# Batch 0's last direct units, earlier up heads and spread transposes in an attention and feed-forward kernel

## The chip, the core and the metric

The kernel runs on one core of a Trainium2 chip. Its time is the device time in microseconds of one execution; several executions give a median. A core has five engines that each run their own list of instructions in order: TensorE (PE, matrix products; PEld is its loading of weights), VectorE (DVE), ScalarE (ACT), GpSimd (POOL) and SyncE (SP). An instruction starts once the instructions of other engines that it depends on are done. Transfers are issued by SP, POOL and ACT, and are carried out by 16 DMA engines.

## The reference

```python
# attention: u, v are (8, 3008, 256), z is (8, 3008, 64)
scores = (1.0 / S) * np.matmul(z, z.transpose(0, 2, 1))
attn = np.maximum(scores, 0.0) ** 2
out = u * np.matmul(attn, v)
# feed-forward: x is out as (24064, 256); w_in is (256, 2048), w_out (2048, 256)
h = x @ w_in
g = h * (1.0 / (1.0 + np.exp(-1.702 * h)))
return g @ w_out
```

There is no softmax: the attention weights are the squares of the positive scores. Since the scores are z times z transposed, the matrix of weights is symmetric.

## The kernel before

A batch has 3008 rows: 24 blocks of 128, the last a half. Four blocks make a chunk of 512 queries, so there are six chunks, i = 0 to 5, the last of 448.

**Scores.** A unit (i, jp) is the score tile of chunk i's queries with two blocks of keys: two matmuls (`scores`, L222), then relu on ACT into `rl` (L246), then the square on DVE into `a` (L260). The tiles `sc` have two buffers in PSUM, which the up groups' `hg` share (the tag `ps2`); `rl` has three buffers, `a` has 21, and the left sums `s` of the feed-forward take theirs from the same 21. In batches 1 to 7 the first unit on a chunk's diagonal writes at L251, and the second (`folded`) is half as wide and writes to `ad` at L244.

**Symmetry.** Only units with keys at or behind the chunk's own are computed. For a later chunk the same square is turned by a DMA transpose from SP (`turn_unit`, L267) into a tile `tt`, one for each pair of chunks. For the last chunk it is done the other way (`turned`, L218): the unit is computed with chunk 5's 512 queries and transposed for the earlier chunk. Where `turned` is false, chunk i computes its units with chunk 5 directly, and chunk 5 computes its own. In batch 0, before, chunks 0 to 2 are direct and chunks 3 and 4 turned.

**Attention.** `attend` (L298) gives a chunk's work as a list of 47 slots, n = 0 to 46. A slot is one or two matmuls `o` with V (L330). In most chunks there are two passes over the blocks, with a slot for the last half block between them (n = 23); there POOL has an empty instruction (`post`, L83) that waits for the first pass and that the second pass waits for. The result is multiplied by the turned u at L347 (`gate`) and is the input `xt` of the feed-forward.

**The order of work** is written by hand: every instruction is placed by the loop over b, i and n at L616 to L648. `SCHED0`, `SCHED`, `SCHED_LAST` and `NEXT` say at which slots of which chunk units are taken from the queue. Chunk 5 of a batch already takes units of the next batch's chunk 0 (`NEXT`). `TURN0` and `TURN` say at which slots u is turned by DVE (L201), `LOAD0` and `LOAD` at which slots POOL issues a load of u; a tile `uq` of u has two buffers, so a load waits for the turning of u two chunks back. `LOADW` places the loads of the weights W1 (L409) and W2 (L412), on POOL as well, and `load_z` the next batch's z, whose cast on POOL waits for its own landing (L160).

**Feed-forward.** An up group (`up_group`, L364) is four matmuls into `hg`, ACT's function into `gf` (L379, two buffers), and a scaling into `gt` on DVE (L383). There are 48 a batch; the first 18 (`LAGY`, the heads) stand between the slots of chunk 4 (chunk 5 in the last batch), the rest each with one product of the down part, `product` (L457), whose outputs SP stores. The down part multiplies by a seven-product scheme, for which DVE forms sums of `gt` (L435) and, in batch 0, sums of W2 (`weight_sums`, L414), one or two after each up group. The tiles `gt` and `tt` share 15 buffers.

**The late transposes.** The transposes of the next batch's chunk 0 units taken in chunk 5 are not issued there but kept in `late`. They are issued after the up groups, one or two after each of the products that remain. The two units taken last are not kept.

Of the kernel before, what the change touches and what calls it, by code (L numbers as in the profile page):

```python
# [15 lines left out]
def kernel(  # L16
# [20 lines left out]
    NJ = (S + P - 1) // P  # L37
# [3 lines left out]
    NCH = (S + CH - 1) // CH  # L41
    CB = CH // P
# [34 lines left out]
    late, LATE = [], []  # L77
# [12 lines left out]
    def behind(sig, m):  # L90
        tc.add_manual_dep(m.ins, sig.ins.name, SYNC, reason="row tiles of one bank")
# [92 lines left out]
    def width(i):  # L184
        return CH if i < NCH - 1 else LAST
# [31 lines left out]

    def turned(b, i):  # L218

        return i < NCH - 1 and (b > 0 or i > 2)  # L220

    def scores(b, group):  # L222
        scs = []
# [53 lines left out]
    def weights(b, i, j):  # L277

        cj, g = divmod(j, CB)
        n = NCH - 1  # L280
        if n in (i, cj) and not turned(b, min(i, cj)):
            return unit[b, i, j // 2][:, j % 2, :width(i)]
        if i < n and cj == n:
            return TT[b, i, n][:, :, g, :]
        if folded(b, i) and cj == i:
            return unit[b, i, j // 2][:, :, g % 2, :]
        if i == n and cj < n:
            return unit[b, cj, NU - 2 + g // 2][:, g % 2, :LAST]
        if cj >= i:
            return unit[b, i, j // 2][:, j % 2, :width(i)]  # L290
        return TT[b, cj, i][:, :, g, :]


    def full(b):

        return NCH - 2 if b < B - 1 else NCH - 1

    def attend(b, i, both=False):  # L298


        n = width(i)
        js, cs = list(range(NJ - 1)), range(2)
        own = i * CB
        if b == 0 and i in (3, 4):
            js = js[own:-CB + 1] + js[:own] + js[-CB + 1:]
        elif b and i == NCH - 3:
            js = js[own:own + 2] + js[own + CB:-CB + 1] + js[:own] + js[own + 2:own + CB] + js[-CB + 1:]
        elif b and i < NCH - 2:
            js = js[own:own + 2] + js[own + CB:-CB + 1] + js[own + 2:own + CB] + js[:own] + js[-CB + 1:]
        half = [(0, TOP, NJ - 1), (1, LOW, NJ - 1)]  # L310
        if both:
            order = [[(c, FULL, j)] for j in js[:-CB] for c in cs] + [[(c, FULL, j)] for c in cs for j in js[-CB:]]
            order.insert(-CB, half)
        elif i == full(b):
            order = [[(c, FULL, j)] for c in cs for j in js]
            order.insert(0 if i == NCH - 1 else len(order), half)
        else:
            order = [[(0, TOP, j), (1, LOW, j)] for j in js] + [half] + [[(1, TOP, j), (0, LOW, j)] for j in js]
        flat = [(k, m) for k, ms in enumerate(order) for m in ms]
        first = {c: next(m for m in flat if m[1][0] == c) for c in cs}  # L320
        final = {c: [m for m in flat if m[1][0] == c][-1] for c in cs}
        acc, turn = {}, -1 if both or i == full(b) else NJ

        def step(k):
            done = []
            for m in order[k]:
                c, h, j = m
                if (k, m) == first[c]:
                    acc[c] = ps1.tile([P, CH], F32, name="o", tag="ps1")
                ins = pe.matmul(  # L330
                    acc[c][:, :n], V16[b][h, j].rearrange("p (c k) -> p k c", k=NCC)[:, c], weights(b, i, j)[h],
                    start=(k, m) == first[c], stop=(k, m) == final[c],
                )
                if k == turn:
                    behind(acc["sig"], ins)
                done.append(ins)
            if k == turn - 1:
                acc["sig"] = post(done)
            for c in cs:
                if k == final[c][0]:  # L340
                    gate(c)

        def gate(c):
            ut = UT[b, i][:, c].rearrange("p q t -> p (q t)")
            x = XT[b, i]
            if i < NCH - 1 or b % 2:
                dve.tensor_tensor(x[:, c, :n], acc[c][:, :n], ut[:, :n], ALU.mult)  # L347
            else:
                dve.tensor_tensor(x[:, c, :LFULL], acc[c][:, :LFULL], ut[:, :LFULL], ALU.mult)
                dve.tensor_tensor(XT[b + 1, i][:, c, LAST:], acc[c][:, LFULL:n], ut[:, LFULL:n], ALU.mult)  # L350

        XT[b, i] = XT.get((b, i)) or pa.tile([P, NCC, CH], F16, name="xt", tag="xt", bufs=6)
        if i == NCH - 1 and b % 2 == 0:
            XT[b + 1, i] = pa.tile([P, NCC, CH], F16, name="xo", tag="xo")
        return [lambda k=k: step(k) for k in range(len(order))]
# [182 lines left out]
            store(b, k, pool)  # L538

    LAGY = 2 * NFG + 2  # L540
    HEAD, HEAD0 = 2, 8

    def pieces(b, i):

# [5 lines left out]
        k = max(len(lst) - 6, 2)  # L550
        return lst[:k] + lst[-2:] + lst[k:-2]

    NEXT = {n: 1 for n in (1, 6, 11, 16, 32, 36, 40, 44)} | {NJ: 2}
    SCHED = {
        0: {n: 1 for n in (4, 8, 12, 16, 20, 28, 32, 36, 40, 44)} | {NJ: 2},
        1: {n: 1 for n in (2, 7, 12, 17)} | {NJ: 2},
        2: {n: 1 for n in (2, 7, 12, 17)} | {NJ: 2},
        3: {n: 1 for n in (6, 14, 32, 38)} | {NJ: 2},
        4: {},
        5: NEXT,  # L560
    }
# [1 line left out]


    TURN0 = {(i, (38, 28)[i] if i < 2 else NJ + 4 if i < NCH - 1 else 12): i for i in range(NCH)}
    LOAD0 = {(i, n): i + 2 for i, n in TURN0 if i + 2 < NCH}
    TURN = {(1, NJ + 4): 2, (2, NJ + 4): 3, (4, NJ + 4): 4, (5, 8): 5}
    LOADW = {(3, 22): 0, (3, 30): 1, (3, 38): 2, (3, 46): 3, (4, 16): 4, (4, 22): 5, (4, 28): 6, (4, 34): 7}
    LOAD = {(3, NJ + 20): 4, (4, NJ + 5): 5}
# [3 lines left out]
        0: {2: 1, 6: 2, 14: 2, 22: 2, 30: 2, 38: 2},  # L573
        1: {0: 2, 8: 2, 15: 2, 22: 2, 30: 2, 38: 2},
        2: {n: 1 for n in (0, 3, 7, 11, 28, 32, 36, 40, 44)} | {NJ: 2},
        3: {n: 1 for n in (3, 7, 11, 15, 19, 28, 32, 36, 40)} | {NJ: 2},
        4: {},
        5: NEXT,
    }
# [7 lines left out]
    def fill(b):  # L587
        assert not queue
        queue.extend(u_ for i in range(NCH) for u_ in pieces(b, i))
# [26 lines left out]
    for b in range(B):  # L616
        nup = NCH * NFG
        more = b + 1 < B
        sched = SCHED0 if b == 0 else SCHED if more else SCHED_LAST
        turn, load = (TURN, LOAD) if b else (TURN0, LOAD0)  # L620
        head, first = 0, HEAD0 if b == 0 else HEAD
        for i in range(NCH):
            host = b + 1 if more and i == NCH - 1 else b
            if host > b:
                fill(host)
                LATE.append(host)
            for n, step in enumerate(attend(b, i, b == 0 and i < 2)):
                if b == 0 and i == 0 and n == 5:
                    load_u(0, 0)
                if b == 0 and i == 0 and n == 3:  # L630
                    turns[1]()
                if b == 0 and i == 0 and n in FIRST_CAST:
                    first_cast(FIRST_CAST[n], True)
                if b == 0 and i == 0 and n in FIRST_ZT:
                    first_zt(FIRST_ZT[n])()
                if (i, n) in turn:
                    turn_u(b, turn[i, n])
                if (i, n) in load:
                    load_u(b, load[i, n])
                if b == 0 and (i, n) in LOADW:  # L640
                    load_w(LOADW[i, n])
                if more and (i, n) == (NCH - 2, 2):
                    load_z(b + 1)
                take(host, sched[i].get(n, 0))
                if i == full(b) and n >= first and (n - first) * LAGY // (2 * NJ - 2 - first) >= head and head < LAGY:
                    up_group(b, head)
                    head += 1
                step()  # L648
        if more:
            for i in range(2):  # L650
                load_u(b + 1, i)
            for n0 in range(0, NJ, VB):
                load_v(b + 1, n0)
        prods = products(nst(b))
        for q in range(head, nup):
            if more and q in (head + 14, head + 20):
                k = int(q == head + 20)
                turn_u(b + 1, k)
                load_u(b + 1, k + 2)
            up_group(b, q)  # L660
            product(b, *prods.pop(0))
        steps = [lambda kp=kp: product(b, *kp) for kp in prods]
        if nst(b) < NCH:
            k = NCH - 1
            steps += [lambda s=s: down(b, k, s) for s in range(blocks(b)[k][1] // P)]
        late.sort(key=lambda t: t[0])
        for step in steps:
            step()
            if SUMS:
                SUMS.pop(0)()  # L670
            for _, turn_it in [late.pop(0) for _ in range(min(len(late), 1 + (len(steps) < 10)))]:
                turn_it()
        LATE.clear()
        if more:
            while late:
                late.pop(0)[1]()
            take(b + 1, 2)
# [30 lines left out]
```

## Time and profile before

| what | value |
|---|---|
| median of 10 executions | 1214.15 us (1208.6 to 1219.31) |
| the profiled execution | 1209.69 us, its span 1207.9 us |
| DVE busy, ACT busy | 823.4 us, 822.4 us |
| `o` matmuls (L330) with `a`, with `tt` | 300.8 us, 235.4 us |
| up matmuls (L371) | 354.7 us |
| down matmuls (L472) | 93.0 + 92.3 + 91.0 us in the three largest groups |
| score matmuls (L232) | 684, 122.1 us |
| transposes `tt` from SP | 234, 3.8 us from issue to landing (median) |
| DMA share in 60 to 90 us, in 120 to 150 us | 0.83, 0.24 |

The page first gives the busy time of each engine and its share of the span. A row of a timeline has the start in us, the duration, the engine, the line, the operation with output and input, and how many equal instructions are drawn together; in brackets stands how long the engine was idle before and what ended that. A row of the waits has the waiting engine and line, what it waited for, the total in us, how many times, and the longest. The durations of matmuls overlap, so a stretch is measured from start to start. A batch takes about 148 us; batch 0 runs from 0 to 170 us with chunk 4 from 65.7, and chunk 5 of batch 1 starts at 242.8.

### The profile page before, as it was taken

The numbers are of one execution on the slowest core, as the hardware profiler recorded it, in microseconds if no ns is written. First come the engines' busy times: TensorE is split into PE (matmuls) and PEld (weight loads), VectorE is DVE, ScalarE is ACT, GpSimd is POOL, SyncE is SP. The second block draws the span as 40 slices with busy tenths as digits, with TensorE's granted clock in tenths as the row PEclk, the third lists the DMA queues.
The fourth block names the chain that finished last, engine by engine and source line by source line (L and its number), as shares of the span: only waits on it lengthen the run. The fifth ranks groups of instructions, "written<-read, shape, count | busy, mean of one in ns | idle before, by whom it ended". The sixth has DMA issues, their size and how long they took to land.

```text
span 1207.9 us, 27521 instructions
## 1 busy us (share of the span) xinstructions
PE 1187.5 (98%) x11423; PEld 715.5 (59%) x11423; DVE 823.4 (68%) x1321; ACT 822.4 (68%) x977; POOL 230.1 (19%) x325
## 2 busy tenths in 40 slices
PE   9998999999999999999999999999999999999998
PEld 3445774467754676446764468544776547855577
DVE  6677855678757785577775778547786577654776
ACT  7776864677646786477864777647876578663785
POOL 5143100331003310123101231013210132101000
PEclk9999999999999999999999999999999999999999
DMA  9987279862898629966299562994539945497012
GB/s 228 188 109 119 74 160 159 98 100 82 153 162 90 111 71 178 155 69 110 71 187 158 60 110 89 193 143 68 91 95 196 137 76 87 116 184 129 1 36 72
DMA packets 375134, 142.33 MB, mean 118 GB/s; under 512 B 317536, under 2 KB 368480, under 8 KB 375008
## 3 DMA queue, kind: packets, MB, share of 16 engines
q1 hardware_dynamic: 316368, 97.30, 44.3%
q0 software_dynamic: 57280, 42.03, 23.0%
q8 instruction: 89, 1.46, 0.5%
q10 hardware_dynamic: 1360, 1.25, 0.3%
q14 instruction: 37, 0.30, 0.1%
HBM read 60.29 MB, written 24.64 MB: 70 GB/s over the span
## 4 chain that ended last, share of the span: by engine, by line
PE 91%; DMA 4%; ACT 2%; DVE 1%; POOL 1%; issue 1%; DVEq 0%; ACTq 0%; POOLq 0%
PE o L330 35%; PE hg L371 26%; PE st L472 23%; PE sc L232 5%; DMA tt<-a 2%; PE yp L528 2%; ACT rl L246 2%; DMA zst<-in_z_dram 1%; DMA W<-in_moe_w_out_dram 1%; DVE a L260 1%; PE w L97 0%; POOL W L412 0%; POOL uq L194 0%; DVE ut L201 0%; ACT ZT L141 0%
## 5 line engine op out<-in xcount | busy, mean ns | idle before, releaser
L379 ACT ACTIVATE gf<-hg 128x1024 f32<-128x1024 f32 (+1 forms) x384 | 385.7, 1004 | 147.0 <-PE hg L371 126.3
L246 ACT ACTIVATE rl<-sc 128x1024 f16<-128x1024 f32 x307 | 302.1, 1026 | 154.7 <-PE sc L232 131.8
L330 PEld LDWEIGHTS <-V 64*128 64x128 f16 (+1 forms) x4052 | 233.2, 94 | 242.9 <-issue 12.5
L371 PE MATMUL hg<-xt,W 128*128 128x512 f16 (+1 forms) x1408 | 354.7, 375 | 1.6 <-DMA W<-in_moe_w_in_dram 0.9
L383 DVE TENSOR_SCALAR gt<-gf 128x1024 f16<-128x1024 f32 (+1 forms) x328 | 231.2, 705 | 134.7 <-ACT gf L379 132.3
L330 PE MATMUL o<-a,V 64*128 64x512 f16 (+3 forms) x2272 | 300.8, 368 | 0.0
L260 DVE TENSOR_TENSOR a<-rl 128x1024 f16<-128x1024 f16 x272 | 186.8, 695 | 149.6 <-ACT rl L246 144.4
L194 POOL DMA_DIRECT2D uq<-in_u_dram x188 | 125.2, 674 | 633.0 <-PE sc L232 299.0
L330 PE MATMUL o<-tt,V 64*128 64x512 f16 (+1 forms) x1524 | 235.4, 377 | 2.7 <-DMA tt<-a 2.6
L371 PEld LDWEIGHTS <-W 128*128 128x128 f16 x1536 | 139.6, 98 | 125.3 <-issue 3.8
L472 PEld LDWEIGHTS <-gt 128*128 128x128 f16 x2816 | 169.1, 98 | 30.4
L472 PEld LDWEIGHTS <-s 128*128 128x128 f16 x2112 | 127.1, 98 | 22.9
L232 PE MATMUL sc<-ZT 64*128 64x512 f16 (+1 forms) x684 | 122.1, 367 | 10.5 <-ACT rl L246 8.7
L472 PE MATMUL st<-WT,gt 128*128 128x128 f16 x1408 | 93.0, 219 | 0.0
L472 PE MATMUL st<-W,gt 128*128 128x128 f16 x1408 | 92.3, 219 | 0.0
L472 PE MATMUL st<-WT,s 128*128 128x128 f16 x1408 | 91.0, 219 | 0.0
L232 PEld LDWEIGHTS <-ZT 64*128 64x128 f16 x684 | 39.9, 94 | 59.6 <-issue 24.3
L488 DVE SCALAR_TENSOR_TENSOR y<-st,uP 128x256 f32<-128x256 f32 x132 | 55.2, 418 | 27.9 <-ACT uP L482 16.6
L482 ACT ACTIVATE uP<-st 128x256 f32<-128x256 f32 x132 | 49.8, 377 | 33.6 <-PE st L472 22.1
L347 DVE TENSOR_TENSOR xt<-o,ut 128x512 f16<-128x512 f32 x80 | 51.4, 684 | 22.8 <-PE o L330 22.8
L447 DVE TENSOR_TENSOR s<-gt,s 128x1024 f16<-128x1024 f16 x88 | 59.6, 681 | 0.0
L445 DVE TENSOR_TENSOR s<-s,gt 128x1024 f16<-128x1024 f16 x88 | 59.6, 682 | 0.0
(51 smaller groups left out, 615.7 us busy)
## 6 DMA issues: line engine op xcount, KB each, us to landing
out_dram<-y SPq DMA_DIRECT2D x40, 512.0 KB, 3.6
uq<-in_u_dram POOLq DMA_DIRECT2D x156, 128.0 KB, 4.3
V<-in_v_dram POOLq DMA_DIRECT2D x35, 256.0 KB, 6.5
tt<-a SPq DMA_TRANSPOSE x234, 3.8
uq<-in_u_dram POOLq DMA_DIRECT2D x32, 112.0 KB, 5.2
vst<-in_v_dram SPq DMA_DIRECT2D x3, 512.0 KB, 6.4
out_dram<-y POOLq DMA_DIRECT2D x4, 384.0 KB, 5.3
zst<-in_z_dram POOLq DMA_DIRECT2D x7, 192.0 KB, 8.2
```

Of the source, the lines that this page charges most:

```text
L194: eng.dma_start(uq[k * QW:(k + 1) * QW, :n // QW].rearrange("t q c k -> t q (c k)"), src[:, :, cs])
L232: pe.matmul(sc[:, r, :m * P], zt[h, 2 * kp + r, :], zt[h, (qi + 1) * CB - m:(qi + 1) * CB, :], start=True, stop=True,)
L246: act.activation(rl, sc, AF.Relu, scale=csc)
L260: dve.tensor_tensor(a, rl, rl, ALU.mult)
L330: ins = pe.matmul(acc[c][:, :n], V16[b][h, j].rearrange("p (c k) -> p k c", k=NCC)[:, c], weights(b, i, j)[h], start=(k, m) == first[c], s ...
L371: pe.matmul(hg[:, e, :n], W1[:, c, ff * P:(ff + 1) * P], XT[b, i][:, c, :n], start=(c == 0), stop=(c == NCC - 1),)
L379: act.activation(gf[:, :, :n], hg[:, :, :n], AF.Gelu_apprx_sigmoid, scale=1.0 / FSC)
L383: dve.tensor_scalar(g, gf[:, :, :n], FSC, None, ALU.mult)
L445: dve.tensor_tensor(s_, ST[b, k, "S1", h], a11, ALU.subtract)
L447: dve.tensor_tensor(s_, a12, ST[b, k, "S2", h], ALU.subtract)
L472: pe.matmul(bank[:, m, :], lhs()[:, f, m, :], right[:, ff, :], start=name in ("P1", "P2", "P5") and m == 0 and ff == 0, stop=ff == NFF // ...
L488: dve.scalar_tensor_tensor(y[:, :, o, c], ST[b, k, "bank" + x], 1.0 / FSC, ST[b, k, "after" + u_], ALU.mult, ALU.add,)
```

## The change

In batch 0, chunk 3 becomes direct: its two units with chunk 5's keys are computed with chunk 3's queries and are not transposed, and chunk 5 computes its two units with chunk 3's keys. Batch 0 then has 50 units and not 48, and chunk 3's slots take 13 and not 11. Chunk 2 of batch 0 begins with its own blocks. The load of u is placed at later slots in batch 0. The heads start at slot 2 in every batch (8 in batch 0 before) and are spread over 38 slots (38 in batch 0, 44 in the others, before). The slots of `NEXT` and of chunk 0 are others. Of the late transposes, one is issued after each odd up group from the 31st on.

```diff
--- before.py
+++ after.py
@@ -217,7 +217,7 @@
 
     def turned(b, i):
 
-        return i < NCH - 1 and (b > 0 or i > 2)
+        return i < NCH - 1 and (b > 0 or i > 3)
 
     def scores(b, group):
         scs = []
@@ -301,7 +301,9 @@
         n = width(i)
         js, cs = list(range(NJ - 1)), range(2)
         own = i * CB
-        if b == 0 and i in (3, 4):
+        if b == 0 and i == 2:
+            js = js[own:own + CB] + js[:own] + js[own + CB:]
+        elif b == 0 and i in (3, 4):
             js = js[own:-CB + 1] + js[:own] + js[-CB + 1:]
         elif b and i == NCH - 3:
             js = js[own:own + 2] + js[own + CB:-CB + 1] + js[:own] + js[own + 2:own + CB] + js[-CB + 1:]
@@ -538,7 +540,7 @@
             store(b, k, pool)
 
     LAGY = 2 * NFG + 2
-    HEAD, HEAD0 = 2, 8
+    HEAD = 2
 
     def pieces(b, i):
 
@@ -550,9 +552,9 @@
         k = max(len(lst) - 6, 2)
         return lst[:k] + lst[-2:] + lst[k:-2]
 
-    NEXT = {n: 1 for n in (1, 6, 11, 16, 32, 36, 40, 44)} | {NJ: 2}
+    NEXT = {n: 1 for n in (3, 8, 13, 17, 31, 36, 41, 46)} | {NJ: 2}
     SCHED = {
-        0: {n: 1 for n in (4, 8, 12, 16, 20, 28, 32, 36, 40, 44)} | {NJ: 2},
+        0: {n: 1 for n in (3, 7, 11, 15, 19, 29, 33, 37, 41, 45)} | {NJ: 2},
         1: {n: 1 for n in (2, 7, 12, 17)} | {NJ: 2},
         2: {n: 1 for n in (2, 7, 12, 17)} | {NJ: 2},
         3: {n: 1 for n in (6, 14, 32, 38)} | {NJ: 2},
@@ -563,7 +565,7 @@
 
 
     TURN0 = {(i, (38, 28)[i] if i < 2 else NJ + 4 if i < NCH - 1 else 12): i for i in range(NCH)}
-    LOAD0 = {(i, n): i + 2 for i, n in TURN0 if i + 2 < NCH}
+    LOAD0 = {(1, 14): 2, (2, 12): 3, (2, NJ + 20): 4, (4, 8): 5}
     TURN = {(1, NJ + 4): 2, (2, NJ + 4): 3, (4, NJ + 4): 4, (5, 8): 5}
     LOADW = {(3, 22): 0, (3, 30): 1, (3, 38): 2, (3, 46): 3, (4, 16): 4, (4, 22): 5, (4, 28): 6, (4, 34): 7}
     LOAD = {(3, NJ + 20): 4, (4, NJ + 5): 5}
@@ -573,7 +575,7 @@
         0: {2: 1, 6: 2, 14: 2, 22: 2, 30: 2, 38: 2},
         1: {0: 2, 8: 2, 15: 2, 22: 2, 30: 2, 38: 2},
         2: {n: 1 for n in (0, 3, 7, 11, 28, 32, 36, 40, 44)} | {NJ: 2},
-        3: {n: 1 for n in (3, 7, 11, 15, 19, 28, 32, 36, 40)} | {NJ: 2},
+        3: {n: 1 for n in (0, 4, 8, 12, 16, 19, 29, 33, 37, 41, 45)} | {NJ: 2},
         4: {},
         5: NEXT,
     }
@@ -618,7 +620,7 @@
         more = b + 1 < B
         sched = SCHED0 if b == 0 else SCHED if more else SCHED_LAST
         turn, load = (TURN, LOAD) if b else (TURN0, LOAD0)
-        head, first = 0, HEAD0 if b == 0 else HEAD
+        head = 0
         for i in range(NCH):
             host = b + 1 if more and i == NCH - 1 else b
             if host > b:
@@ -642,10 +644,11 @@
                 if more and (i, n) == (NCH - 2, 2):
                     load_z(b + 1)
                 take(host, sched[i].get(n, 0))
-                if i == full(b) and n >= first and (n - first) * LAGY // (2 * NJ - 2 - first) >= head and head < LAGY:
+                if i == full(b) and n >= HEAD and (n - HEAD) * LAGY // (2 * NJ - 10) >= head and head < LAGY:
                     up_group(b, head)
                     head += 1
                 step()
+        late.sort(key=lambda t: t[0])
         if more:
             for i in range(2):
                 load_u(b + 1, i)
@@ -659,11 +662,12 @@
                 load_u(b + 1, k + 2)
             up_group(b, q)
             product(b, *prods.pop(0))
+            if q >= 30 and q % 2 and late:
+                late.pop(0)[1]()
         steps = [lambda kp=kp: product(b, *kp) for kp in prods]
         if nst(b) < NCH:
             k = NCH - 1
             steps += [lambda s=s: down(b, k, s) for s in range(blocks(b)[k][1] // P)]
-        late.sort(key=lambda t: t[0])
         for step in steps:
             step()
             if SUMS:
```

## The prediction

> **What bounds the kernel now.** I read the page's busy shares first, then the waits of TensorE alone, then the timelines around the places where those waits lie. A batch is b (0 to 7), a chunk i (0 to 5), a slot n (0 to 46) of a chunk's attention, a unit (i, jp) one score tile with its relu and square, an up group q.
>
> ```profile
> PE 1187.5 (98%) x11423; PEld 715.5 (59%) x11423; DVE 823.4 (68%) x1321; ACT 822.4 (68%) x977; POOL 230.1 (19%) x325
> ...
> PE sc L232 <- ACT rl L246: 8.7, 14, 2.5
> PE o L330 <- DMA tt<-a: 2.6, 4, 1.7
> ...
> PE hg L371 <- DMA W<-in_moe_w_in_dram: 0.9, 1, 0.9
> ...
> PE hg L371 <- ACT gf L379: 0.7, 1, 0.7
> ...
> PE sc L232 <- ACT gf L379: 0.4, 1, 0.4
> ```
>
> TensorE is the bound: 98% busy, clock full in every slice. So only two things count: matmuls added, and TensorE's waits (total us, times, longest). Those five rows sum to 13.3 us; about 3 us more lie in the first 16 us, which the change leaves alone. Nothing it does can gain more than 13.3. Where they lie, TensorE's rows with the idle time before each:
>
> ```profile
> 58.26 1.04 PE L330 MATMUL o<-tt,V 64*128 64x512 f16 x8 [1.67 <-DMA tt<-a]
> ...
> 71.31 1.04 PE L371 MATMUL hg<-xt,W 128*128 128x512 f16 x4 [0.90 <-DMA W<-in_moe_w_in_dram]
> ...
> 102.25 0.39 PE L232 MATMUL sc<-ZT 64*128 64x512 f16 x2 [2.53 <-ACT rl L246]
> ...
> 250.74 0.39 PE L232 MATMUL sc<-ZT 64*128 64x512 f16 x2 [0.51 <-ACT rl L246]
> ...
> 252.34 0.39 PE L232 MATMUL sc<-ZT 64*128 64x512 f16 x2 [0.45 <-ACT rl L246]
> ```
>
> The pair 0.51 + 0.45 returns in chunk 5 of batches 1 to 6 (5.7 us of the 8.7); batch 0 holds the rest, at 102.25 and 0.48 at 106.58. The other three `tt` waits (0.21, 0.22, 0.48 in batches 3, 5, 7) close the 2.6.
>
> **The change, part by part.** Sums are against the profiled execution (1209.69 us, span 1207.9).
>
> *Chunk 3's last units direct (batch 0).* The rows of 58.26 are chunk 3's blocks 20 to 23, whose weights come as transposed tiles: that transfer took 8.45 us in the chain of waits. Direct units need no transfer: −1.67. Nothing is late in its place: the same units then stand in chunk 2's slots 36 and 40, half a chunk ahead of their use. Chunk 5 must compute two units of its own: two score pairs, each moving its neighbours apart by 0.22 us on TensorE: +0.43, uncovered. The two relus (1.03 us) and squares (0.7) are hidden: chunk 3 now carries 13 units in 47 slots and 13 score pairs of 0.216 (an up group's four matmuls pitch at 0.865, so one at 0.216), 13.0 us, and ACT's pitch in a run of five relus is (4.69 − 1.02)/4 = 0.92, so 12.0 us. That cover is thin; gone, it would cost up to 1 us.
>
> *u loads later (batch 0).* In the built program's order the loads of chunks 2, 3 and 4 stand at the same places of POOL's queue behind the same releases (the `ut` transposes): they start when they did, cost 0. Only chunk 5's load moves, on POOL, from between the first and second W1 load to behind the z loads and ahead of the four W2 loads.
>
> ```profile
> 63.67 2.55 POOL L194 DMA_DIRECT2D uq<-in_u_dram  x4 [11.40 <-DVE ut L201]
> 66.22 2.12 POOL L409 DMA_DIRECT2D W<-in_moe_w_in_dram  x3
> ```
>
> POOL stood 11.40 us at it with W1 queued behind. Now W1's last three wait only for the middle of chunk 3 (58.26 + 0.86 before; less 1.67, and one score pair more: 57.7), so they are issued 8.5 us earlier. Chunk 4 began at 65.70 and begins 1.24 earlier (1.67 − 0.43); up group 2, two slots and two groups of 1.32 later, is at 67.5 and finds the second W1 load landed even at 8.0 us, the slowest weight load of the trace: −0.90. z follows, then u (2.6 us of issue), then W2: its last issue goes from 88.3 to about 84: 8.5 earlier as z is, its landings (7.25 and 5.93 us) kept, 2.6 given back to u's issue, and 1.5 that I keep for fuller queues.
>
> *Heads six slots earlier in batch 0, and ending at slot 38 to 40 everywhere.* Batch 0 keeps its pace (38 slots for 18 groups), but starts at n = 2. What stops TensorE at 102.25 is a chain through DVE:
>
> ```profile
> 92.92 0.69 DVE L418 TENSOR_TENSOR WT<-W 128x1024 f16<-128x1024 f16 x1 [1.29 <-DMA W<-in_moe_w_out_dram]
> ...
> 95.58 0.69 DVE L419 TENSOR_TENSOR WT<-W,WT 128x1024 f16<-128x1024 f16 x1 [1.37 <-DMA W<-in_moe_w_out_dram]
> ```
>
> DVE stands 2.66 us for W2, its first square of chunk 5 slips to 100.40, ACT lacks a free `rl`, TensorE a free `sc`. Demand moves too: chunk 4 is 1.24 earlier, the heads 1.3 (six slots), W1's wait 0.9, and the 0.75 at 87.99 mostly gone: some 4.4 earlier (the two-sum groups still make DVE late), so DVE asks for W2 at 87.2 (was 91.63), then at 89.8. [...] The trace's W2 loads took a median of 6.8 us and the chain shows 7.15: landing near 88.5 (92.92 − 4.4) and 91, DVE waits 1.3 and 1.2 again. [...] TensorE stood ready for the sixth score of chunk 5 at 99.72 and is now there 1.24 + 1.3 + 0.9 + 0.4 earlier, at 95.9; the buffer comes with DVE's last wait, 4.5 before 102.25, at 97.8: 1.9 left, and 0.3 of the 0.75: −1.9 (bounds 0 and −4.1). In batches 1 to 6 the heads close from 1.40 to 1.32 us a group, against ACT 1.02 and DVE 0.605 + 0.605; the 1.24 us `ut` between them makes DVE late by about 1.2, and about 1.75 is needed before TensorE stands (1.0 to the second `gf`, 0.74 to the second `hg`). Cost 0, bound +1.1 each, what batch 0 lost at that pace (0.75 + 0.38).
>
> *Chunk 5's slots in batches 1 to 6.* The pair of waits is no backlog of the heads:
>
> ```profile
> 249.21 0.42 DVE L244 TENSOR_TENSOR ad<-rl 128x512 f16<-128x512 f16 x1 [2.79 <-PE o L330]
> 249.55 1.10 DVE L201 STREAM_TRANSPOSE ut<-uq 128x896 f32<-128x896 f32 x1
> 250.58 2.45 DVE L260 TENSOR_TENSOR a<-rl 128x1024 f16<-128x1024 f16 x4
> ...
> 249.66 1.02 ACT L246 ACTIVATE rl<-sc 128x1024 f16<-128x1024 f32 x1 [1.83 <-DVE ad L244]
> 251.26 4.69 ACT L246 ACTIVATE rl<-sc 128x1024 f16<-128x1024 f32 x5 [0.57 <-DVE a L260]
> ```
>
> The second unit's square waits for an `a` buffer that slot 25 of the same chunk frees; the changed program has the same wait. The seventh score is tied to it: square, relu, 250.74. It now stands at slot 31, not 32: 0.19 less work ahead of it, wait 0.51 → 0.70. But the `ut` transpose (1.10 us) now stands ahead of that square, because u's slot 8 has become the second unit's, and runs while DVE idles; u landed some 9 us before (issued by 233.8, 6.2 at most to land). The third square no longer waits for it, so the eighth score's buffer is free at about 251.7, and TensorE arrives at 251.9: 0.45 → 0. Net −0.26, six times: −1.6 (bounds +1.1 and −5.7, the whole of it more or less).
>
> *Chunk 0's transposes spread (batches 1 to 7).* Before, eight stand on SP after the last product, and hold it past the next batch's start:
>
> ```profile
> 456.43 13.25 SPq L272 DMA_TRANSPOSE tt<-a  x8
> ```
>
> 1.66 us each. [...] The row says SP is behind until chunk 0's end, and TensorE stood 0.91 for `tt`. I take the row: −0.91. In the up stretch a transpose comes every 3.5 us, DMA is at 0.45 there, stores of 3.6 us fit between; each new `tt` takes a `gt` freed at least 83 matmuls before. Cost 0.
>
> *Batch 0's chunk 2 order and the other slots*: no wait of before stands there; moved, not added: 0.
>
> **Sum**: −1.67 + 0.43 − 0.90 − 1.9 − 1.6 − 0.9 = **−6.5 us**. The profiled time would be 1203.2; its run lies 4.5 below the median of ten, so the median goes from 1214.15 to **1207.6**.
>
> **Rivals.** (A) *All the waits go*: W2 comes early enough and the slots hide slot 25's chain: −12.9 (13.3 without the 0.43 added): 1201.3. For: what is queued ahead of W2 gets shorter. Against: the wait on slot 25 stays in the program. (B) *Waits move only*: W2's contention with u takes back batch 0's 1.9 and W1's 0.9, and the seventh score's 0.19 is all that chunk 5 sees (+1.1): −1.67 + 0.43 − 0.91 + 1.1 = −1.0: 1213.1. For: it was DMA's landing that was late, and those loads are the same bytes. (C) *Slower*: the closer heads make DVE the bound in batches 1 to 6, deciding once DVE is over 1.75 us late; each then loses what batch 0 lost at that pace, 1.1, and no gain in chunk 5: 6.8 − 0.91 − 1.67 + 0.43 − 0.9 = +3.8: 1218. For: batch 0 did stand. Against: it drew two sums a group, these draw one. That the loads of u start no later is the part of the title that does not happen.
>
> **Chances.** Forecast 0.52 (1205 to 1210.4), A 0.14, B 0.22, C 0.12. The range 1202 to 1214 holds the forecast's, most of A and B's lower side. 0.3% (3.6 us) is what a measurement can tell: faster takes forecast and A, 0.66; same is B, 0.22; slower C, 0.12.
>
> **What would show it.** `tt` waits gone from TensorE's list; no wait for W1; DVE's two waits for W2 near 1 us each and a shorter one at the sixth score; in chunk 5 one wait of 0.7 in place of two; W1 issued before 60. Wrong, if TensorE waits for `gf` in batches 1 to 6, if ACT's chunk 3 row stops TensorE before chunk 4, or if chunk 5's pair stays at 0.96.

## The result and the profile after

| | before | after |
|---|---|---|
| median | 1214.69 us (32 executions, 1206.05 to 1219.31) | 1202.41 us (9 executions, 1200.4 to 1207.45) |
| the profiled execution | 1209.69 us, span 1207.9 | 1203.5 us, span 1201.7 |

The ratio is 0.9915, with a 95% interval of 0.9893 to 0.9936: 10.3 us faster (7.8 to 13.0); the two medians alone lie 12.3 apart. (The record lists a tenth execution of the changed kernel, of 1209.6 us, which the nine leave out; with it the median would be 1202.96.) From profile to profile it is only 6.2 us. The forecast for the profiled time was 1203.2, for the median 1207.6. So the sum was right to 0.3 us, in part because its errors cancel, and the median lay 5.2 below what was made of it. Most of the study is about that difference.

First the page's row of engines after, then TensorE's waits (total us, times, longest):

```profile
PE 1186.2 (99%) x11427; PEld 724.9 (60%) x11427; DVE 825.2 (69%) x1323; ACT 825.1 (69%) x979; POOL 232.2 (19%) x325
```

```profile
PE sc L232 <- ACT rl L246: 7.7, 14, 1.7
PE hg L373 <- ACT gf L381: 1.5, 4, 0.8
PE w L97 <- DVE nil L75: 1.2, 1, 1.2
```

Four matmuls, two relus and two squares came with chunk 5's own units of batch 0. The rows for `tt` and for W1 are gone. The `rl` row still counts 14 waits, but they are other ones. TensorE's timeline after, with start, duration and idle time before each:

```profile
87.80 1.02 PE L373 MATMUL hg<-xt,W 128*128 128x512 f16 x4 [0.78 <-ACT gf L381]
99.40 0.39 PE L232 MATMUL sc<-ZT 64*128 64x512 f16 x2 [1.72 <-ACT rl L246]
167.25 0.39 PE L232 MATMUL sc<-ZT 64*128 64x512 f16 x2 [0.25 <-ACT rl L246]
235.28 1.02 PE L373 MATMUL hg<-xt,W 128*128 128x512 f16 x4 [0.18 <-ACT gf L381]
247.40 0.39 PE L232 MATMUL sc<-ZT 64*128 64x512 f16 x2 [0.70 <-ACT rl L246]
```

The sixth score of chunk 5 in batch 0 waits 1.72 where it waited 2.53. The 0.70 is the only wait in chunk 5 of batch 1, and it comes back in each of the batches 1 to 6. New are 0.25 us at the third score of chunk 0, seven times, and 0.18, 0.31 and 0.17 us for `gf` in the heads of batches 1, 3 and 5. VectorE's timeline around W2, and then around chunk 5 of batch 1:

```profile
90.03 0.69 DVE L420 TENSOR_TENSOR WT<-W 128x1024 f16<-128x1024 f16 x1 [0.99 <-DMA W<-in_moe_w_out_dram]
...
92.73 0.69 DVE L421 TENSOR_TENSOR WT<-W,WT 128x1024 f16<-128x1024 f16 x1 [1.41 <-DMA W<-in_moe_w_out_dram]
...
242.45 1.10 DVE L201 STREAM_TRANSPOSE ut<-uq 128x896 f32<-128x896 f32 x1
245.86 0.43 DVE L244 TENSOR_TENSOR ad<-rl 128x512 f16<-128x512 f16 x1 [2.32 <-PE o L332]
246.24 1.29 DVE L260 TENSOR_TENSOR a<-rl 128x1024 f16<-128x1024 f16 x2
```

W2 is still late, by 2.40 in place of 2.66 us. The turning of u runs while VectorE would idle, ahead of the square that it used to hold up; that square still waits 2.32 us for slot 25. GpSimd's rows show the W1 loads issued at 59.16, and the W2 loads at 82.16:

```profile
59.16 2.10 POOL L411 DMA_DIRECT2D W<-in_moe_w_in_dram  x3 [5.99 <-PE sc L232]
61.26 1.02 POOL L156 DMA_DIRECT2D zst<-in_z_dram  x1
...
79.47 2.69 POOL L194 DMA_DIRECT2D uq<-in_u_dram  x4
82.16 3.94 POOL L414 DMA_DIRECT2D W<-in_moe_w_out_dram  x4
```

And SyncE's queue in the up stretch of batch 1, where the block of eight stood before, now has them between the stores:

```profile
280.87 7.42 SPq L272 DMA_TRANSPOSE tt<-a  x3
292.37 0.37 SPq L516 DMA_DIRECT2D out_dram<-y  x1
292.83 6.27 SPq L272 DMA_TRANSPOSE tt<-a  x4
```

To see where the time went, I compared the start of the same ACT row (the `gf` of an up group) in two traces. The table has after minus before, in us, at the first and the last up group of each batch:

| batch | 0 | 1 | 2 | 3 | 4 | 5 | 6 | 7 |
|---|---|---|---|---|---|---|---|---|
| first up group | −1.48 | −3.68 | −3.77 | −4.10 | −4.35 | −5.03 | −5.12 | −6.20 |
| last up group | −3.50 | −3.78 | −3.72 | −4.10 | −4.65 | −5.13 | −5.55 | −6.20 |

Batch 0 gives 3.5, though the changed execution was late before any edit could act: ACT's sixth relu starts at 12.63 us against 11.61 before, and VectorE's first `xt` row, at the end of chunk 0, at 25.11 against 24.21. From there on batch 0 gains 4.4. Between batches (chunks 0 to 3 of batches 1 to 7) the steps from one column's last to the next one's first sum to 1.8; within batches 1 to 6 (chunks 4 and 5) to 0.9.

### The profile page after: what moved, and what is told of

The parts are those of the page before. It is cut to its first block, busy times and chain, and to the rows that moved or that the text cites. A ratio compares the mean times of both kernels' runs of the same rounds, so it can differ in the third digit from the quotient of the medians.

```text
span 1201.7 us, 27542 instructions
## 1 busy us (share of the span) xinstructions
PE 1186.2 (99%) x11427; PEld 724.9 (60%) x11427; DVE 825.2 (69%) x1323; ACT 825.1 (69%) x979; POOL 232.2 (19%) x325
## 4 chain that ended last, share of the span: by engine, by line
PE 90%; DVE 3%; ACT 2%; DMA 2%; issue 1%; POOL 1%; DVEq 0%; ACTq 0%; POOLq 0%
PE o L332 36%; PE hg L373 24%; PE st L474 23%; PE sc L232 6%; PE yp L530 2%; ACT rl L246 1%; DMA zst<-in_z_dram 1%; DVE gt L385 1%; ACT gf L381 1%; DMA W<-in_moe_w_out_dram 1%; DVE s L445 1%; DVE ut L201 0%; PE w L97 0%; POOL W L414 0%; DVE s L447 0%
## 5 line engine op out<-in xcount | busy, mean ns | idle before, releaser
L332 PEld LDWEIGHTS <-V 64*128 64x128 f16 (+1 forms) x4052 | 241.4, 94 | 232.6 <-issue 12.1
L332 PE MATMUL o<-a,V 64*128 64x512 f16 (+3 forms) x2286 | 304.0, 368 | 0.0
L445 DVE TENSOR_TENSOR s<-gt 128x1024 f16<-128x1024 f16 x88 | 59.9, 696 | 0.0
```

The source lines that it names most:

```text
L332: ins = pe.matmul(acc[c][:, :n], V16[b][h, j].rearrange("p (c k) -> p k c", k=NCC)[:, c], weights(b, i, j)[h], start=(k, m) == first[c], s ...
L445: dve.tensor_tensor(s_, a21, a22, ALU.add)
```

## The experiments

Each kernel ran in five rounds beside the kernel before. The first four shared one chip, the last four another. The theory was that the parts add up, and that the wait for `tt` in batch 0 differs between executions; the rival was that one part carries the gain and the rest is noise.

**The control: before again.** Only a constant is written otherwise.

```diff
-    LAGY = 2 * NFG + 2
+    LAGY = 2 + 2 * NFG
```

> The kernel before once more, the same instructions. Ratio 1.000 within the interval. Its profile shows another execution: if its time is nearer to the median than 1209.69, the theory that tt waits differ from execution to execution (B) expects longer tt waits in it than 2.6 us in all; the theory that the executions differ in the first 20 us alone (the loads at the start) expects the same tt waits and a later first up group.

Ratio 0.9989 (0.9965 to 1.0013), median 1214.48, but the profiled execution had a span of 1212.9. Its waits of TensorE, the row of its timeline, and its windows (us, busy of PE, PEld, DVE, ACT, POOL with instructions, granted clock, DMA share, GB/s):

```profile
PE o L330 <- DMA tt<-a: 7.4, 4, 5.4
```

```profile
61.90 1.89 PE L330 MATMUL o<-tt,V 64*128 64x512 f16 x8 [5.38 <-DMA tt<-a]
```

```profile
60.00:65.00 5.00, 3.10 (x16) 1.16 (x18) 0.00 (x0) 0.75 (x1) 0.00 (x0) 0.66 1.13 234
```

The same program waited 5.38 us at the place where the profile of before showed 1.67, and its clock was 0.66 in the 5 us in which that wait ended. Its start was that of before (the first `xt` row at 24.13 us against 24.21), so what made this execution longer does not lie in the first 20 us. So the 1.67 of the prediction was one draw of a number that varies.

**The spread alone.** Chunk 0's late transposes go to the last up groups; nothing else.

```diff
             product(b, *prods.pop(0))
+            if q >= 30 and q % 2 and late:
+                late.pop(0)[1]()
```

> The kernel before with the late transposes alone spread over the up groups. The prediction's sum: the tt waits of batches 3, 5 and 7 (0.91 us) go from TensorE's list, the 1.67 of batch 0 stays, the span falls by 0.9 us, a ratio of 0.999. Theory B (SP's backlog costs a typical execution much more than the one profiled, and is where the median moved beyond the profile): 4 to 7 us less, a ratio of 0.994 to 0.997. Theory C (the backlog was hidden): no change of the ratio.

Ratio 0.9963 (0.9938 to 0.9988), median 1209.9: 4.5 us by the ratio, where the sum had 0.9, just outside the interval. No wait for `tt` stands in batches 1 to 7 any more. From the last up group of batch 0 to the end it gained 1.8 us on before, all of it in chunks 0 to 3, as in the changed kernel; the listed waits that went are 0.91. The stretch from a batch's last up group to the next one's first lasts 59.5, 60.5 or 69.6 us here, and to 0.02 us the same in the three other kernels with the spread (changed, and the last two below). In the kernels without it the seven stretches together are 0.8 to 2.9 us longer, each execution in its own way: 1.9 in the profile of before, 2.9 in the control, where one wait for `tt` in batch 6 is 1.14. The profile shows what is left in batch 0, this time in chunk 2:

```profile
42.16 1.46 PE L330 MATMUL o<-tt,V 64*128 64x512 f16 x6 [2.81 <-DMA tt<-a]
```

**Batch 0 alone.** Chunk 3 direct with its slots, chunk 2's order, u's loads, the heads from slot 2.

```diff
-        return i < NCH - 1 and (b > 0 or i > 2)
+        return i < NCH - 1 and (b > 0 or i > 3)
...
-    LOAD0 = {(i, n): i + 2 for i, n in TURN0 if i + 2 < NCH}
+    LOAD0 = {(1, 14): 2, (2, 12): 3, (2, NJ + 20): 4, (4, 8): 5}
```

> The kernel before with batch 0's edits alone: chunk 3 direct, chunk 2's order, u's load, heads from slot 2. Batches 1 to 7 as before. The prediction's sum: 1.67 + 0.90 + 1.9 - 0.43 = 4.0 us less, a ratio of 0.9967; no wait for W1 and for tt in batch 0; the sixth score of chunk 5 waits 1.9 or more (here chunk 5's slots are the old ones). Theory B (batch 0 is saturated with DMA, so a typical execution loses more there than the profiled one did): 6 us or more, 0.995 or less.

Ratio 0.9952 (0.9925 to 0.9979), median 1208.66, span 1202.4. No wait for W1, 0.5 us for `tt` in all, none of it in batch 0, and 4.65 us gained by the last up group of batch 0. VectorE waited 0.19 and 1.41 us for W2, and the sixth score 0.92, where 1.9 or more was expected. The interval holds both the sum (0.9967) and the theory's 0.995.

**Two halves of it.** The direct chunk 3 with its slots (Direct), and, apart from it, u's loads with the heads from slot 2 (Order).

```diff
-    HEAD, HEAD0 = 2, 8
+    HEAD, HEAD0 = 2, 2
```

> The kernel before with chunk 3 of batch 0 direct and its 13 slots, and nothing else of batch 0. Theory B1 (the wait for chunk 3's transposed tiles is 1.67 in a lucky execution and 5 to 8 us in others, with a low granted clock behind it, and is where the median moved beyond the profile): no tt wait at the end of chunk 3's first pass, the granted clock 1.00 in all of batch 0, a median 4 to 6 us below the kernel before, a ratio of 0.9950 to 0.9967. The rival (that wait is 1.67 nearly always, the rest is W1's and W2's loads): 1.2 us less, a ratio of 0.999. A tt wait in chunk 2, as the first experiment's 2.81, may stay in either.

> The kernel before with the place of u's load and batch 0's heads from slot 2 alone; chunk 3 stays turned. The prediction's sum: W1's wait (0.90) gone and 1.3 to 1.9 less at the sixth score, 2.2 to 2.8 us less, a ratio of 0.998. Theory B1: the tt wait in chunk 3 stays and varies, so that the median is no more than 3 us below. The rival (loads): 4 us or more.

Direct: 0.998 (0.9954 to 1.0006), median 1211.32. Its profile has 0.3 us for `tt`, in batch 5. W1's wait has grown to 1.63: its last three loads were issued 1.7 us earlier (64.50 for 66.22), as chunk 4 was, but the first of them took 5.8 us to land, where it took 5.0 before. Order: 0.9968 (0.9944 to 0.9992), median 1209.86; no wait for W1. The product of the two, 0.9948, agrees with the 0.9952 of both with chunk 2's order: within the intervals the parts add, and of chunk 2's order nothing is seen.

Both results lie on the rival's side of what was expected. Direct should have given 4 to 6 us if chunk 3's wait for `tt` were where the median moved beyond the profile; it gave 2.4 by the ratio (5.6 less to 0.7 more). Order should then have given no more than 3; it gave 3.9 (1.0 to 6.8). The intervals are too wide to settle it. Nor does chunk 3, which is still turned in Order, wait in this profile. Its row of TensorE's waits (the one wait lies in batch 1) and its first windows:

```profile
PE o L330 <- DMA tt<-a: 0.2, 1, 0.2
```

```profile
0.00:10.00 10.00, 7.06 (x33) 2.36 (x33) 4.81 (x13) 5.33 (x6) 3.26 (x10) 0.87 0.85 269
10.00:20.00 10.00, 9.75 (x46) 3.17 (x45) 5.04 (x7) 8.15 (x13) 8.90 (x12) 0.79 1.17 251
```

The clock was low in the first 20 us (0.87 and 0.79), and the first `xt` row came at 26.84 us, 2.6 later than before, while SyncE began its long run of transposes at 16.79 (17.32 before). A start so late leaves the transposes 2.6 us more; whether it or the edit took the wait away, this profile does not tell.

**The other slots alone.** `NEXT`, chunk 0's slots, and the heads' end at slot 38.

```diff
-    NEXT = {n: 1 for n in (1, 6, 11, 16, 32, 36, 40, 44)} | {NJ: 2}
+    NEXT = {n: 1 for n in (3, 8, 13, 17, 31, 36, 41, 46)} | {NJ: 2}
```

> The kernel before with the slots alone: heads over 38 slots, NEXT's and chunk 0's slots. The prediction's sum: in chunk 5 of batches 1 to 6 one wait of 0.70 in place of 0.51 and 0.45, 1.6 us less in all, a ratio of 0.9987; the 0.18 to 0.31 waits for gf that the changed kernel shows in odd batches should be here too and take back some 0.7. The rival that the heads are too close: no gain, or up to 2 us more.

Ratio 0.9988 (0.996 to 1.0016). The profiled execution, span 1214.3, was the unluckiest seen; its timeline, and its windows:

```profile
65.13 1.89 PE L330 MATMUL o<-tt,V 64*128 64x512 f16 x8 [8.28 <-DMA tt<-a]
```

```profile
60.00:65.00 5.00, 0.00 (x0) 0.00 (x0) 0.00 (x0) 0.00 (x0) 0.00 (x0) 0.50 1.31 139
65.00:70.00 5.00, 4.87 (x24) 1.78 (x26) 1.23 (x2) 1.94 (x2) 0.00 (x0) 0.50 0.93 182
```

From 60 to 65 us none of the engines that compute did anything while the DMA share read 1.31; TensorE's row says that it stood for the transfer of `tt`. The edit touches nothing before that place. From chunk 4 to the first up group after chunk 5 this kernel gained 0.11, −0.03, 0.01, 0.30, 0.10 and 0.44 us in batches 1 to 6, and the changed kernel 0.10, −0.05, 0, 0.30, 0.10 and 0.43: 0.9 in all in both, batch by batch to 0.02 us. It is not quite a constant: the next kernel, with the same slots and heads in these batches, gained 0.18, 0.11, 0.34, 0.30, 0.09 and 0.30, 1.3 in all.

**u's load behind W2.** The changed kernel with chunk 5's load of u at slot 36 of chunk 4.

```diff
-    LOAD0 = {(1, 14): 2, (2, 12): 3, (2, NJ + 20): 4, (4, 8): 5}
+    LOAD0 = {(1, 14): 2, (2, 12): 3, (2, NJ + 20): 4, (4, 36): 5}
```

> The changed kernel with chunk 5's load of u behind the W2 loads, at slot 36 of chunk 4. If W2's landing is what makes DVE late: W2 is issued 2.7 us earlier, DVE's two waits (0.99 and 1.41) fall below 0.3 together, the sixth score's wait falls from 1.72 to below 0.3, the 0.78 for gf ahead of it stays; batch 0 ends 1.5 to 1.9 us earlier. If the landing is set by contention and not by the issue: the waits stay within 0.5.

Ratio to before 0.9895 (0.9865 to 0.9925), median 1202.05. VectorE does not wait for W2, and the sixth score does not wait; the 0.78 for `gf`, expected to stay, is 0.39. But a wait for `tt` in chunk 2 took the gain back in the profiled execution:

```profile
43.63 1.07 PE L332 MATMUL o<-tt,V 64*128 64x512 f16 x6 [2.88 <-DMA tt<-a]
```

So a long wait for `tt` can still occur with chunk 3 direct. It also blurs the test: chunk 4 came 3.8 us later, and W2 was issued 10.1 us after the first up group's ACT row in place of 15.1. Of these 5.0 us the edit accounts for 2.7, the time that u's load took to issue in the changed kernel (2.69 us, at 79.47); that the rest comes from z, ahead of W2 in GpSimd's queue, is an inference that no landing time here shows. By the times the edit's worth is not told from nothing.

**The seventh score's slot.** The changed kernel with chunk 5's later units at 35, 38, 42 and 46.

```diff
-    NEXT = {n: 1 for n in (3, 8, 13, 17, 31, 36, 41, 46)} | {NJ: 2}
+    NEXT = {n: 1 for n in (3, 8, 13, 17, 35, 38, 42, 46)} | {NJ: 2}
```

> The changed kernel with chunk 5's last slots at 35, 38, 42 and 46 in place of 31, 36, 41 and 46. If the seventh score waits for a chain that starts at slot 25: the 0.70 of batches 1 to 6 goes (four slots of 0.19 are 0.75), each batch is 0.65 shorter, 4 us in all, a ratio of 0.9966 to the changed kernel. If it is ACT's backlog, a wait of 0.3 or more stands at the eighth to tenth score or at the first up group after the chunk in its place.

Ratio to before 0.989 (0.9855 to 0.9924), median 1199.22, span 1196.3: the lowest of all, though the interval overlaps that of the changed kernel. TensorE's waits in it:

```profile
PE sc L232 <- ACT rl L246: 2.0, 8, 0.3
PE hg L373 <- ACT rl L246: 1.3, 6, 0.2
```

The 0.70 is gone six times, and the first up group after chunk 5 gives 0.22 of it back. Measured at the up groups, 2.8 us were gained on the changed kernel in batches 1 to 6, a mean of 0.46 each where 0.65 was expected. The other 2.6 fell in batch 0, which the edit does not touch: there VectorE waited only 0.44 for W2, with the loads issued in the same order as in the changed kernel. So the run before this one doesn't show that the order of issue decides W2's landing; what differs from one execution to the next does as much.

Not tried: the two last edits together, the changed kernel with the spread or the direct chunk 3 taken back, and the earlier end of the heads without the slots.

## Why the prediction was right for the profile and short for the median

**The step that failed is the last one, "its run lies 4.5 below the median of ten, so the median goes from 1214.15 to 1207.6".** It took the 4.5 us as a constant between a profiled execution and the median. They are what the profiled execution did not suffer: the changed kernel's profiled execution lies 1.1 above its median. For the same reason the 13.3 us that "nothing it does can gain more than" bound one execution alone; the last run's median lies 15.1 below. Each execution lists its mean granted clock, and that tells the two kinds apart:

| kernel | executions | mean clock | at full clock (1.000) | median at full clock | median of all |
|---|---|---|---|---|---|
| before, beside the first four | 34 | 0.9971 | 3 | 1208.6 | 1214.81 |
| before, beside the last four | 23 | 0.9973 | 1 | 1207.26 | 1214.35 |
| control | 12 | 0.9970 | 0 | | 1214.48 |
| the other slots alone | 12 | 0.9968 | 1 | 1207.84 | 1214.57 |
| spread alone | 12 | 0.9979 | 2 | 1207.76 | 1209.9 |
| direct alone | 12 | 0.9978 | 2 | 1206.91 | 1211.32 |
| u's loads and heads alone | 12 | 0.9980 | 1 | 1215.21 | 1209.86 |
| batch 0 alone | 11 | 0.9985 | 3 | 1205.98 | 1208.66 |
| changed | 9 | 0.9990 | 4 | 1201.54 | 1202.41 |
| changed, u behind W2 | 5 | 0.9992 | 2 | 1201.07 | 1202.05 |
| changed, seventh score | 6 | 0.9988 | 3 | 1198.55 | 1199.22 |

The profile of before is one with the clock full in every slice; of these 57 executions of before only 4 were so: 1206.77, 1207.26, 1208.6 and 1209.69, with 1207.9 in their middle. The changed kernel's four lie at 1201.54. At full clock, then, the change is worth 6.4 us, from four executions on each side that spread over 3 us, and the sum had said 6.5. The other 5.9 us of the medians' difference go with executions at a lower clock: 53 of 57 before, 5 of 9 after. Five of the traced executions had a lower clock, and it fell in different places: at chunk 3's wait for `tt` in the control and the other slots alone (down to 0.66 and 0.50 in a window of 5 us), at a wait for `tt` in chunk 2 in the spread alone and with u behind W2 (0.83 in 10 us in both), and at the start (0.87 and 0.79) and the sixth score of chunk 5 (0.83) in Order. So chunk 3's wait is one source among several, and what the executions without a trace met stays open. By an estimate from these clocks and times, a mean clock of 0.9972 is worth at most 0.0028 × 1213 = 3.4 us, less where it was low while TensorE stood anyway, and the waits themselves come on top. One execution doesn't fit: of the kernel with u's loads and heads alone, 1215.21 us at full clock. It has no trace, and its cause stays open.

That the sum met the profile to 0.3 us is in part luck. Against its terms the changed execution lost 0.9 us at the start, where nothing was edited, gained 0.4 more in batch 0 and 0.9 more by the spread, and gained 0.7 less in chunk 5.

**Chunk 3 direct: mechanism right, its worth to the median open.** The term was −1.67. Up to that place before, the spread alone, the slots alone and the control issue the same instructions, and their longest waits for `tt` in batch 0 were 1.67, 2.81 (in chunk 2), 8.28 and 5.38 us: a mean of 4.5. With chunk 3 direct five profiles (changed, batch 0 alone, direct alone, and the last two) had 0, 0, 0, 2.88 and 1.17, the last two in chunk 2: a mean of 0.8. So the profiles show chunk 3's own wait gone and chunk 2's left. The difference of the means, 3.7, is 2.0 more than the term, but it rests on nine draws that overlap, and Order, turned and without a wait in batch 0, speaks against a fixed size. The times of Direct do not show more than the term either. How the median's surplus splits between this, the loads and the spread, the intervals are too wide to tell. The two extra units cost no wait, as forecast.

**W1: right.** Its loads were issued at 59.16 (57.7 forecast) and the wait is gone. **W2: right.** VectorE was to wait 1.3 and 1.2 and waited 0.99 and 1.41; the sixth score was to wait 1.9 and waited 1.72. The landings of before held: W2's four loads took 5.0 to 7.3 us here, with a median of 6.6, and 5.2 to 7.1 with a median of 6.8 before. That the waits themselves came out so near is luck: with the same order of issue VectorE waited 1.60 us in all for W2 in batch 0 alone and 0.44 in the last run, against 2.40 here. The `gf` wait before it was mis-sized: 0.3 forecast, 0.78 found at 87.80. It comes before VectorE's first wait for W2, so W2 is not its cause; the two-sum groups that make VectorE late, which moved along with the heads, are the likely one. Four waits of before, 0.75 and 0.38 for `gf` and 2.53 and 0.48 for `rl`, make the 4.1 that bounds the term (4.14); 1.64 of them were gained, not 1.9.

**Chunk 5 of batches 1 to 6: right in each wait, short in the sum.** 0.51 and 0.45 became 0.70 and 0, with u's turning ahead of the square as worked out. The forecast was −1.6; the marks give −0.9. The heads, put at nothing, brought the 0.18, 0.31 and 0.17 for `gf`: 0.66 together, and in those batches (1, 3 and 5) the marks show 0.10, 0 and 0.10 gained. Batch 2, with −0.05, has the same wait in two pieces of 0.12 and 0.04, too short for the list; batches 4 and 6, without it, gained 0.30 and 0.43, more than the forecast's 0.26. So the term that was wrong is the heads' 0, and a wait for `gf` in these batches was one of the prediction's own signs of being wrong. The cost lay within its bound of 1.1 each.

**The spread: right, and too small.** The waits for `tt` are gone. The term was 0.91; the marks give 1.8, in the spread alone and in the changed kernel alike. Half of it stood in no listed wait of before: where a wait of 0.21, 0.22 or 0.48 went, the stretch became 0.38, 0.39 and 0.65 shorter, and two stretches without one 0.18 and 0.25. What these rests were stays open. Since the stretches without the spread differ from execution to execution, 1.8 is again one draw; of the kernels without it, before lies between the extremes of 0.8 and 2.9. The third score's 0.25 seven times was not foreseen. It costs nothing: the spread alone has no such wait, and its seven stretches are as long as the changed kernel's to 0.02 us.

**The rivals.** Waits that only move would have left W2's gain and W1's at nothing; both came, W2's with the luck described. Heads that make VectorE the bound: its sign is there, 0.17 to 0.31 us where its price was 1.1. All waits gone: those of VectorE for W2, of the sixth score and of the seventh stayed.

## What to carry to other kernels

Before a profile's sum is put on a median, look whether the profiled execution was a typical one: the granted clock of every execution is the quickest sign (4 of 57 executions of before ran at full clock, the profiled one among them), and the gap to the median, 4.5 us here, is a term of its own, which a change can remove. A wait on a transfer can be a distribution, not a number: chunk 3's wait for `tt` took 1.67, 5.38 and 8.28 us in three executions with the same instructions up to it, with a DMA share of 1.15, 1.29 and 1.26 in the window of 55 to 60 us. Take its size from several executions, or bound it upwards. The pair of waits on one buffer chain was moved here, not removed (0.51 and 0.45 became 0.70 and 0): following which slot frees which buffer gave the new waits to 0.3 us.

## What the hardware showed unasked

The clock fell after waits of very different lengths. It was 0.50 in the window of 65 to 70 us, after TensorE's wait of 8.28 us (the other slots alone; and in 60 to 65 already, while TensorE stood), and 0.66 in that of 60 to 65, in which the wait of 5.38 ended (the control). The eight matmuls behind either wait took 1.89 us; the same eight took 1.04 behind the wait of 1.67 before, at a clock of 1.00. After 2.81 us (spread alone) and 2.88 us (u behind W2) it was 0.83 in the window of 40 to 50 us, after 2.57 us (Order, at 101.89) 0.83 in 100 to 110. The row of the spread alone:

```profile
40.00:50.00 10.00, 7.80 (x58) 3.16 (x60) 2.25 (x5) 3.46 (x5) 0.00 (x0) 0.83 1.24 179
```

In the last four the loss is the same, 0.34 of 5 us or 0.17 of 10: 1.7 us of clock. A wait of 1.74 us (the control, at 106.23) left the clock at 1.00 in 100 to 110 us, and so did the longest of before, 2.53 at 102.25. At the start of Order TensorE was busy for 1.3 of the 3 us from 5 to 8, with no single wait above 0.83 there, and the clock was 0.87 in the first 10 us and 0.79 in the next 10: four matmuls at 10.32 took 1.89 us, eight of the same form at 22.00 took 1.90. So the length of a wait alone does not decide. Part of the price of such a wait thus comes after it, as in the 1.89 us in place of 1.04.
